# Five instead of six work pairs behind the first two scores of a run, and fewer double periods, in a fused attention and SwiGLU kernel

## The chip, the cores and the metric

The kernel runs on one core of a Trainium2 chip. The metric is the device time of one launch in microseconds (us); for the kernel before it is the median of three runs. Beside the times there is one profiled execution with its trace, from which all durations below come.

The engines of a core run side by side and wait for each other through semaphores: TensorE (PE in the profile; its weight loads are listed apart as PEld), VectorE (DVE), ScalarE (ACT), GpSimd (POOL), and SyncE (SP), which here mostly issues DMAs. What stands on one engine runs in the order in which the program wrote it.

## The reference

One sequence of 2048 rows with 512 features goes through two branches, which are mixed row by row by a gate. The batch dimension of 1 is left out below.

```python
g = sigmoid((x * gate_w).sum(-1, keepdims=True))
# branch a: attention with 32 heads of 16 features
qkv = (x @ wqkv).reshape(S, 3, 32, 16)          # q, k, v
p = softmax(q @ k.T * 16 ** -0.5)               # per head, 2048 x 2048
a = (p @ v) @ wo
# branch b: SwiGLU, hidden size 1792
b = (silu(x @ w1) * (x @ w3)) @ w2
out = g * a + (1 - g) * b
```

All inputs and the output are float32.

## The kernel before

**Attention in units.** Two heads are taken together, so there are 16 head pairs, and the 2048 queries are taken in two halves: 32 steps, each with one head pair and one half. A step has 16 blocks of 128 keys times two groups of 512 queries, that is 32 units, and there are 1024 units in all. One unit is:

- a score (letter Q, `score`, line 888): two matmuls, one for each head, with 50 rows of K as weights and 512 queries moving. The one sits in the upper half of the array's rows and the other in the lower half, so they run at the same time. They fill one of the two PSUM buffers named S (128 x 2 x 512);
- an exponential on ACT (line 892), over those 1024 columns at once, from S into a tile p in SBUF (twelve of them in rotation, four of which are named v). It follows the score in program order;
- two matmuls with V (line 875), p moving and 17 columns of V as weights, which add to the PSUM bank acc. The letter P (`pv`) does this for the two oldest pending units: four matmuls, which take four strips of the array's columns side by side. In the trace each such matmul is two records.

Since there are two S buffers, a score can only start when the exponential of the score two before it has been read out. The wait is on the score's weight load, which the trace lists under PEld and which in undisturbed work begins before the matmuls that stand ahead of it have ended.

**Work pairs.** Everything else that TensorE has to do (the rest of the projections, the three SwiGLU products, the output product) is cut into blocks whose contraction is split over the two halves of the array's rows. `feed()` (letter F) issues the next matmul of each half: a work pair, two matmuls of 64 rows by 512 columns that run side by side (lines 460, 584, 674, 681). Which block is next depends on how many letters have gone by (`clock`), since a bank must have been read by VectorE before it is written again.

**The order.** TensorE's program is a string of these letters, walked once at build time. A run of n units is

```python
run = lambda n, m=6: "QQ" + "F" * m + "QFFF" * (n - 3) + "Q" + "P" * (n // 2)
```

so two scores, m work pairs, then one score for each three work pairs, a last score, and all products with V of the run. The kernel has four runs of 8, then 15 times a run of 12 and two runs of 10 (32 units: one step), then `LONG` runs of 8, called long periods here. After them come `SHORT` double periods of 8 units (`two`), in which the products with V come in two groups with two scores between them:

```python
two = "QFFF" * 5 + "QPPQQPP"
```

A group of P stands between scores and work pairs in every run, one group in a long period and two in a double one. DMAs for the next step's K and Q (`load_step`), and the vector work on gates and sums, hang on the number of scores issued and of blocks done.

Of the kernel before, what the change touches and what calls it, by code (L numbers as in the profile page):

```python
# [17 lines left out]
P = 128  # L18
S = 2048
D = 512  # L20
F = 1792
# [13 lines left out]
def gated_mix_kernel(ctx: ExitStack, tc: tile.TileContext, x, wqkv, wo, w1, w3, w2, gate_w, out):  # L35
# [861 lines left out]


    NP = 8
    THIRDS, LONG, SHORT = 16, 35, 28  # L900
    run = lambda n, m=6: "QQ" + "F" * m + "QFFF" * (n - 3) + "Q" + "P" * (n // 2)
    two = "QFFF" * 5 + "QPPQQPP"
    order = run(8) * 4 + (run(12) + run(10) * 2) * (THIRDS - 1) + run(8) * LONG + "QQ" + "F" * 7 + two * SHORT + "QFFF" * 5 + "QPPPP"
    MORE = ["v0", "v1", "v2", "v3"]
    free = list(range(NP))

# [127 lines left out]
```

## Time and profile before

| | |
|---|---|
| median of 3 runs | 1396.81 us (1395.8 to 1397.53) |
| the profiled execution | 1396.22 us, of which 1394.4 us is the span from the first to the last instruction |
| PE | 1386.5 us busy, 99% of the span |
| PEld | 836.8 us, 60% |
| ACT | 1025.1 us, 74% |
| DVE | 491.5 us, 35% |
| POOL | 335.8 us, 24% |
| granted TensorE clock | 1.00 throughout |

Read the rows of the timeline so: start in us from the span's start, duration in us, engine, line, operation, tiles written and read, shape, how many such instructions follow one another, and in brackets the idle time of the engine ahead of them with what ended it. PE's busy time overlaps: a matmul is shown from its start to its (modelled) end, and the next one starts before that. What TensorE's work costs is therefore read from the distance between starts, and not from durations.

### The profile page before, as it was taken

The page shows a single profiled execution, that of the slowest core. Times are in us where ns is not written, and L with a number is a line of the kernel's source. Part 1 is how long each engine was busy: PE and PEld are TensorE (multiplying, and loading weights), DVE is VectorE, ACT ScalarE, POOL GpSimd, SP SyncE. Part 2 cuts the span into 40 slices and gives each one's busy share as a digit, 9 for nine tenths or more (in the row PEclk, how much of TensorE's full clock was granted, in tenths as well). Part 3 has the DMA queues.
Part 4 walks back from the last instruction along what each step waited for, and adds up shares of the span by engine and source line. Part 5 has one row for each costly group of instructions (what it writes and reads, how often), then busy time and mean ns, then how long its engine had stood idle before and what let it go on. Part 6 is the DMA issues. An engine that isn't in the chain of part 4 may idle for free.

```text
span 1394.4 us, 29335 instructions
## 1 busy us (share of the span) xinstructions
PE 1386.5 (99%) x11601; PEld 836.8 (60%) x11601; DVE 491.5 (35%) x1101; ACT 1025.1 (74%) x1151; POOL 335.8 (24%) x371
## 2 busy tenths in 40 slices
PE   9999999999999999999999999999999999999998
PEld 8766565656566565656565566566566555555554
DVE  6411111446464646564555545431111110110113
ACT  5467677777778677778777777777677787887884
POOL 6104344210111011101110114543253431232402
PEclk9999999999999999999999999999999999999999
DMA  9505455532323233332233424536534554444632
GB/s 272 139 10 144 98 145 142 120 94 62 77 71 91 60 80 78 76 86 71 62 78 77 107 67 108 122 107 124 110 105 91 118 123 88 96 100 98 162 110 84
DMA packets 111186, 141.30 MB, mean 101 GB/s; under 512 B 16422, under 2 KB 69414, under 8 KB 108066
## 3 DMA queue, kind: packets, MB, share of 16 engines
q1 hardware_dynamic: 109888, 137.40, 40.7%
q8 instruction: 93, 1.52, 0.5%
q10 hardware_dynamic: 1154, 1.97, 0.4%
q14 instruction: 51, 0.42, 0.1%
HBM read 90.69 MB, written 48.61 MB: 100 GB/s over the span
## 4 chain that ended last, share of the span: by engine, by line
PE 95%; DVE 1%; issue 0%; DVEq 0%
PE acc L875 33%; PE f L460 27%; PE S L888 19%; PE f L584 11%; PE f L674 2%; PE f L760 1%; PE f L681 1%; DVE xH L686 0%; DVE xL L686 0%; PE f L960 0%; DVE sg L497 0%; PE S L960 0%; DVE u L949 0%; DVE sg L515 0%; PE S L971 0%
## 5 line engine op out<-in xcount | busy, mean ns | idle before, releaser
L892 ACT ACTIVATE p<-S 128x1024 f32<-128x1024 f32 x864 | 817.2, 1027 | 273.6 <-PE S L888 272.2
L888 PE MATMUL S<-Qt,Kt 50*128 50x512 f32 x2048 | 409.9, 407 | 1.2 <-SPq L316 1.1
L875 PE MATMUL acc<-p,V 128*17 128x512 f32 x3456 | 400.8, 594 | 0.0
L888 PEld LDWEIGHTS S<-Qt,Kt 50*128 50x128 f32 x2048 | 187.8, 184 | 153.7 <-issue 73.0
L875 PEld LDWEIGHTS acc<-p,V 128*17 128x17 f32 x3456 | 88.7, 97 | 235.8 <-issue 235.1
L497 DVE RECIPROCAL sg<-sg 128x64 f32<-128x64 f32 x448 | 209.6, 518 | 52.6 <-issue 48.6
L460 PE MATMUL f<-xH,fl 64*128 64x512 f32 x1104 | 223.8, 394 | 0.1
L460 PE MATMUL f<-xH,fh 64*128 64x512 f32 x1104 | 221.6, 389 | 0.0
L460 PE MATMUL f<-xL,fh 64*128 64x512 f32 x1104 | 221.2, 389 | 0.0
L892 ACT ACTIVATE v<-S 128x1024 f32<-128x1024 f32 x160 | 153.0, 1027 | 54.7 <-PE S L888 54.4
L460 PEld LDWEIGHTS f<-xH,fh 64*128 64x128 f32 x1104 | 108.6, 184 | 23.3 <-DVE tick L847 0.2
L460 PEld LDWEIGHTS f<-xL,fh 64*128 64x128 f32 x1104 | 109.1, 187 | 22.4
L351 POOL CAST fh<-fr 128x512 fp32r<-128x512 f32 x35 | 22.1, 631 | 416.7 <-DMA fr<-in_B_w_dram 368.1
L460 PEld LDWEIGHTS f<-xH,fl 64*128 64x128 f32 x1104 | 108.8, 186 | 22.2 <-DVE raw L511 0.5
L847 DVE MEMSET tick<- 1x1 f32 x205 | 12.1, 59 | 310.4 <-PE f L584 152.5
L875 PE MATMUL acc<-v,V 128*17 128x512 f32 x640 | 77.1, 593 | 0.0
L584 PE MATMUL f<-xL,fh 64*128 64x512 f32 x208 | 66.2, 390 | 0.0
L584 PE MATMUL f<-xH,fl 64*128 64x512 f32 x208 | 65.9, 390 | 0.0
L584 PE MATMUL f<-xH,fh 64*128 64x512 f32 x208 | 61.2, 390 | 0.0
L857 DVE COPY u<-acc 128x512 f32<-128x512 f32 x31 | 21.5, 692 | 102.3 <-PE acc L875 102.3
L489 DVE COPY gs<-f 128x512 f32<-128x512 f32 x56 | 38.4, 687 | 53.2 <-PE f L460 52.4
L495 DVE TENSOR_SCALAR sg<-sg 128x512 f32<-128x512 f32 x56 | 26.1, 466 | 88.1 <-ACT sg L494 84.8
(221 smaller groups left out, 1417.2 us busy)
## 6 DMA issues: line engine op xcount, KB each, us to landing
Kt<-kH_d SPq DMA_DIRECT2D x124, 128.0 KB
h_d<-sg SPq DMA_DIRECT2D x56, 256.0 KB
sg<-h_d SPq DMA_DIRECT2D x43, 256.0 KB
fr<-in_B_w_dram SPq DMA_DIRECT2D x42, 256.0 KB
Qt<-qH_d SPq DMA_DIRECT2D x128, 64.0 KB
Kt<-kL_d SPq DMA_DIRECT2D x62, 128.0 KB
Qt<-qL_d SPq DMA_DIRECT2D x64, 64.0 KB
b_d<-yy SPq DMA_DIRECT2D x16, 256.0 KB
```

The source lines that it names most:

```text
L351: nc.gpsimd.tensor_copy(hi, src)
L460: return nc.tensor.matmul(ps, w[i == 1][r, k, :], (xL if i == 2 else xH)[b][r, k, :], start=n == 0 and not second, stop=n == 3 * ND - 1 an ...
L489: nc.vector.tensor_copy(gs, ps)
L495: small.append(lambda: nc.vector.tensor_scalar(sg, sg, 1.0, None, op0=OP.add))
L497: small.append(lambda q=q: nc.vector.reciprocal(sg[:, q:q + 64], sg[:, q:q + 64]))
L584: ins = nc.tensor.matmul(ps, hs[t][q][i == 1][r, P * o:P * o + P], (w2L if i == 2 else w2H)[q][r, o, :], start=n == 0 and not second, stop ...
L674: return nc.tensor.matmul(ps, ot[t][i == 1][r, P * k:P * k + P], wo_[k][i == 2][r, :], start=n == 0 and not second, stop=n == 3 * ND - 1 a ...
L681: return nc.tensor.matmul(ps, o_rows(t, k, i == 1)[r, :], wo_[k][i == 2][r, :], start=n == 0 and not second, stop=n == LATE - 1 and (secon ...
L857: nc.vector.tensor_copy(u, acc)
L875: nc.tensor.matmul(acc[r:r + DH + 1, :], V[:, k, 2 * j + h, :], p[:, h, :], start=k == 0, stop=k == NT - 1)
L888: nc.tensor.matmul(ps[:, h, :], Kt[i][r:r + 50, P * k:P * k + P], Qt[i][r:r + 50, t:t + 512], start=True, stop=True)
L892: nc.scalar.activation(p, ps, AF.Exp, scale=SCALE)
```

## The change

`run` gets five work pairs by default behind its first two scores. The four runs of the first step keep six. The pairs that this sets free, 45 in the runs of 12 and 10 and one in each long period, go where 16 double periods were: these become long periods, with 20 work pairs each instead of 15.

```diff
     NP = 8
-    THIRDS, LONG, SHORT = 16, 35, 28
-    run = lambda n, m=6: "QQ" + "F" * m + "QFFF" * (n - 3) + "Q" + "P" * (n // 2)
+    THIRDS, LONG, SHORT = 16, 51, 12
+    run = lambda n, m=5: "QQ" + "F" * m + "QFFF" * (n - 3) + "Q" + "P" * (n // 2)
     two = "QFFF" * 5 + "QPPQQPP"
-    order = run(8) * 4 + (run(12) + run(10) * 2) * (THIRDS - 1) + run(8) * LONG + "QQ" + "F" * 7 + two * SHORT + "QFFF" * 5 + "QPPPP"
+    order = run(8, 6) * 4 + (run(12) + run(10) * 2) * (THIRDS - 1) + run(8) * LONG + "QQ" + "F" * 7 + two * SHORT + "QFFF" * 5 + "QPPPP"
```

Scores, products with V and letters F are as many as before, counted from the string:

| stage | runs before | F before | runs now | F now |
|---|---|---|---|---|
| first step, runs of 8 | 4 | 84 | 4 | 84 |
| runs of 12 | 15 | 495 | 15 | 480 |
| runs of 10 | 30 | 810 | 30 | 780 |
| long periods (8 units) | 35 | 735 | 51 | 1020 |
| double periods (8 units) | 28 | 420 | 12 | 180 |
| the rest | | 22 | | 22 |
| sum | | 2566 | | 2566 |

Groups of P: 4 + 45 + 35 + 2 x 28 + 1 = 141 before, 4 + 45 + 51 + 2 x 12 + 1 = 125 now.

The first place is on TensorE in the second step, in the first run that the change reaches, around its third score. The pieces of the difference show work pairs (line 460, f<- a half of x and a half of a weight) and the score (line 888).

```order
 L460 MATMUL f<-xL_159,fh_5878 128x512
 L460 MATMUL f<-xL_479,fh_5872 128x512
+L888 MATMUL S<-Qt_109,Kt_112 128x512 x2
 L460 MATMUL f<-xH_158,fh_5878 128x512
 L460 MATMUL f<-xH_478,fh_5872 128x512
-L888 MATMUL S<-Qt_109,Kt_112 128x512 x2
```

The third score moves ahead of one work pair, and so does each later score of the run; the pair itself comes right behind it, ahead of the next score.

The second place is on TensorE at about the 870th of the 1024 units. Before, it lies in the double periods: two groups of products with V (line 875) with two scores between them.

```order
L888 MATMUL S<-Qt_109,Kt_112 128x512 x2
L875 MATMUL acc<-p_19348,V 17x512 x2
L875 MATMUL acc<-p_19353,V 17x512 x2
L875 MATMUL acc<-p_19376,V 17x512 x2
L875 MATMUL acc<-p_19387,V 17x512 x2
L888 MATMUL S<-Qt_109,Kt_112 128x512 x4
L875 MATMUL acc<-p_19404,V 17x512 x2
L875 MATMUL acc<-p_19423,V 17x512 x2
L875 MATMUL acc<-p_19448,V 17x512 x2
L875 MATMUL acc<-p_19469,V 17x512 x2
L888 MATMUL S<-Qt_109,Kt_112 128x512 x2
```

With the change the same stretch lies in the long periods: the eight units' products come in one group, and the next run's first two scores stand behind all of them.

```order
L888 MATMUL S<-Qt_109,Kt_112 128x512 x2
L875 MATMUL acc<-p_19487,V 17x512 x2
L875 MATMUL acc<-p_19492,V 17x512 x2
L875 MATMUL acc<-p_19508,V 17x512 x2
L875 MATMUL acc<-p_19525,V 17x512 x2
L875 MATMUL acc<-p_19544,V 17x512 x2
L875 MATMUL acc<-p_19555,V 17x512 x2
L875 MATMUL acc<-p_19576,V 17x512 x2
L875 MATMUL acc<-p_19587,V 17x512 x2
L888 MATMUL S<-Qt_109,Kt_112 128x512 x4
```

There is one change between scores and products in place of two for these eight units, and the two scores that stood between the groups now stand at a run's head.

## The prediction

> **What bounds the kernel now.** I read the page first: the busy times, the shares of the chain that ended last, and the two groups that the change touches.
>
> ```profile
> PE 1386.5 (99%) x11601; PEld 836.8 (60%) x11601; DVE 491.5 (35%) x1101; ACT 1025.1 (74%) x1151; POOL 335.8 (24%) x371
> ...
> PE 95%; DVE 1%; issue 0%; DVEq 0%
> ...
> L892 ACT ACTIVATE p<-S 128x1024 f32<-128x1024 f32 x864 | 817.2, 1027 | 273.6 <-PE S L888 272.2
> L888 PE MATMUL S<-Qt,Kt 50*128 50x512 f32 x2048 | 409.9, 407 | 1.2 <-SPq L316 1.1
> ```
>
> TensorE is the bound, and 95% of the last chain lies on it. A busy PE does not say that it runs at its beat, though: a score that waits for its buffer shows under PEld, at its weight load. So the waits of PEld come next, and beside them those of ACT on itself.
>
> ```profile
> PEld S L888 <- issue: 73.0, 85, 1.5
> PEld S L888 <- ACT p L892: 49.8, 65, 0.9
> ACT p L892 <- ACT p L892: 0.7, 4, 0.2
> ACT v L892 <- ACT v L892: 0.3, 2, 0.2
> ACT p L892 <- ACT v L892: 0.2, 1, 0.2
> ```
>
> The first two rows look like 123 us of waiting and are mostly something else. 85 is the number of all groups of P outside the double periods (141 - 56), and 73.0 / 85 is 0.86 us each: the weight loader is idle behind a group of P, since the products keep the array. The double periods' 56 groups make 56 x 0.86 = 48 of the 49.8 us in the second row, put down to ACT only because its signal came last. What is left for real waits on an exponential is about 2 us. So today TensorE hardly ever waits for ACT, and its time is the number of its items times their beat, plus what it costs to go from scores to products and back. Both are read from the timeline, from one group of P to the same place of the next period: a long period, then a double one.
>
> ```profile
> 945.12 3.63 PE L875 MATMUL acc<-p,V 128*17 128x512 f32 x32
> ...
> 950.64 0.40 PE L888 MATMUL S<-Qt,Kt 50*128 50x512 f32 x2
> ...
> 955.28 0.39 PE L888 MATMUL S<-Qt,Kt 50*128 50x512 f32 x2
> 955.60 3.63 PE L875 MATMUL acc<-p,V 128*17 128x512 f32 x32
> ```
> ```profile
> 1122.44 1.91 PE L875 MATMUL acc<-p,V 128*17 128x512 f32 x16
> ...
> 1124.95 1.91 PE L875 MATMUL acc<-p,V 128*17 128x512 f32 x16
> ...
> 1131.85 1.91 PE L875 MATMUL acc<-p,V 128*17 128x512 f32 x16
> ```
>
> From 950.64 to 955.28 there are 20 items (5 scores, 15 work pairs): 4.64 / 20 = 0.232 us an item. A long period takes 955.60 - 945.12 = 10.48 us for 8 scores, 21 pairs and 4 P, a double one 1131.85 - 1122.44 = 9.41 us for 8 scores, 15 pairs and 4 P. Six pairs fewer should save 6 x 0.232 = 1.39 us, and only 1.07 are saved: the second group of P (at 1124.95) costs 0.32 us.
>
> **Part one: fewer groups of P.** All letters stay as many as they were (1024 scores, 2566 F, 512 P), so the items' beat alone gives no change. Groups of P go from 141 to 125: 16 x 0.32 = 5.1 us less, on the engine that sets the end. This is the whole possible gain.
>
> **Part two: the third score comes one pair sooner, in 96 runs** (45 of 12 and 10 units, 51 long periods). Whether its buffer is free by then is the question. The head of a run with six pairs:
>
> ```profile
> 711.59 0.73 PE L888 MATMUL S<-Qt,Kt 50*128 50x512 f32 x4
> 712.19 3.82 ACT L892 ACTIVATE p<-S 128x1024 f32<-128x1024 f32 x4 [4.16 <-PE S L888]
> 713.32 0.19 PEld L888 LDWEIGHTS S<-Qt,Kt 50*128 50x128 f32 x2
> 713.55 0.40 PE L888 MATMUL S<-Qt,Kt 50*128 50x512 f32 x2
> 713.78 0.40 PE L460 MATMUL f<-xH,fl 64*128 64x512 f32 x2
> ```
>
> The first exponential starts at 712.19 and, at the page's mean of 1.027, ends at 713.22. The third score's weight load goes out at 713.32, 0.10 us later, and the next work pair starts at 713.78, 0.46 us after the load. With five pairs the load would be due at 713.09, and the buffer is not free. What a late exponential does to a score stands elsewhere, where ACT paused and the loads met it:
>
> ```profile
> 717.96 0.19 PEld L888 LDWEIGHTS S<-Qt,Kt 50*128 50x128 f32 x2
> 718.03 1.94 ACT L892 ACTIVATE v<-S 128x1024 f32<-128x1024 f32 x2 [0.17 <-ACT v L892]
> 718.19 0.39 PE L888 MATMUL S<-Qt,Kt 50*128 50x512 f32 x2
> 718.42 0.40 PE L460 MATMUL f<-xH,fl 64*128 64x512 f32 x2
> ...
> 719.11 0.19 PEld L888 LDWEIGHTS S<-Qt,Kt 50*128 50x128 f32 x2 [0.26 <-ACT v L892]
> 719.12 0.49 PE L888 MATMUL S<-Qt,Kt 50*128 50x512 f32 x2
> ...
> 719.45 0.39 PE L460 MATMUL f<-xH,fl 64*128 64x512 f32 x2
> ```
>
> The exponential that began at 718.03 ended at 719.06, and the load went out at 719.11: 0.05 us behind. From this load to the next pair it is 0.34 us instead of 0.46, so a late load gives 0.12 us of its lead back; the pair comes at 719.45 where four items after 718.42 it would have been 719.35. By these numbers the third score with five pairs loads at 713.22 + 0.05 = 713.27, and the pair behind it starts at 713.61 instead of 713.78 - 0.23 = 713.55. 0.06 us is lost at each run's third score, between 0.05 and 0.06 within the rows' last digit: 96 x 0.055 = **5.3 us** (4.8 to 5.8), which alone takes back the 5.1.
>
> **Part three: the rest of such a run.** From the third score on the loads go out right behind the exponentials, with no lead. Two trains of before ran in this way, one behind another pause of ACT and one in the last run, where too few pairs stood ahead of a score:
>
> ```profile
> 642.78 7.44 ACT L892 ACTIVATE p<-S 128x1024 f32<-128x1024 f32 x8 [0.20 <-ACT v L892]
> 643.86 0.19 PEld L888 LDWEIGHTS S<-Qt,Kt 50*128 50x128 f32 x2 [0.26 <-ACT p L892]
> ...
> 644.89 0.40 PE L888 MATMUL S<-Qt,Kt 50*128 50x512 f32 x2
> ...
> 648.63 0.40 PE L888 MATMUL S<-Qt,Kt 50*128 50x512 f32 x2
> ```
> ```profile
> 1372.22 5.62 ACT L892 ACTIVATE p<-S 128x1024 f32<-128x1024 f32 x6 [0.57 <-PE S L888]
> ...
> 1373.30 0.19 PEld L888 LDWEIGHTS S<-Qt,Kt 50*128 50x128 f32 x2 [0.45 <-ACT p L892]
> ...
> 1374.34 0.39 PE L888 MATMUL S<-Qt,Kt 50*128 50x512 f32 x2
> ...
> 1376.21 0.39 PE L888 MATMUL S<-Qt,Kt 50*128 50x512 f32 x2
> ```
>
> Eight exponentials in 7.44 us follow one another every (7.44 - 1.03) / 7 = 0.916 us, less than a score and three pairs take undisturbed (718.19 - 713.55 over 5 intervals: 0.928), so ACT catches up by itself and no second wait follows. But the scores come every (648.63 - 644.89) / 4 = 0.935 us in the first train and (1376.21 - 1374.34) / 2 = 0.935 in the second: 0.008 more than 0.927 to 0.928. I can't say from the trace why, and take it as measured, for all intervals but the first behind a wait. After the third score a run of 8 has 5 intervals, one of 10 has 7, one of 12 has 9: 51 x 4 + 30 x 6 + 15 x 8 = 504, times 0.008 is **4.0 us**. The ends are 0 (the extra is chance in two trains) and 600 x 0.008 = 4.8.
>
> The Trainium skill speaks harder against the change. Its page "ScalarE: Activation LUTs", section "What ACT_TABLE_LOAD costs", gives an activation with immediate operands 186 ns + 0.833 ns a column and lets neighbours overlap by 93 ns; by an estimate from that page, 1024 columns would follow one another every 0.946 us, more than TensorE's 0.927, and with no slack left each of the 600 intervals would lose 0.019: 11.4 us in place of 4.0, and 1408.5 us in all. The two trains' 0.916 above, and 1.94 - 1.03 = 0.91 for the pair at 718.03, don't bear that out.
>
> **Part four: ACT's pauses.** The waits of ACT on itself list 4 + 2 + 1 = 7 pauses of up to 0.2 us. Before, one cost 0.10 on PE, as at 719.45. With no lead in hand it costs its whole 0.2 where more scores of the run follow: 7 x 0.1 = 0.7 us more (0 to 1.9, were each 0.27).
>
> What moves without a price: the pairs from 16 double periods lie in long periods now, with the same beat; VectorE's and GpSimd's work and SP's loads for the next step hang on the same counts and change places by single items, covered by a DVE at 35% and by loads that no row of the waits names ahead of a score. If that cover were gone, a score would show a wait on a DMA.
>
> **The sum.** Against the profiled execution's own 1396.22 us: -5.1 + 5.3 + 4.0 + 0.7 = +4.9, so **1401.1 us**. The ends are -5.1 + 4.8 = -0.3 (1395.9) and -5.1 + 5.8 + 4.8 + 1.9 = +7.4 (1403.6). The profiled execution lies 0.6 below the median of 1396.81, well inside the runs' 1395.8 to 1397.53.
>
> **The rivals.**
> - *The wait alone.* The third score is late, but later scores keep 0.928 and pauses cost as before: -5.1 + 5.3 = 1396.4, up to 1397.1 with the pauses. For it: 0.008 comes from six intervals in two trains. Against: both trains show the same 0.935. Chance 0.22.
> - *No wait at all, and faster.* The place is the weight load of the third score, the price is nothing, and all of the 5.1 stays: 1391.1. It decides if the first exponential ends 0.06 us sooner against the scores, for instance if the load could follow its end at once and not by 0.05. For it: a late load already gives back 0.12. Against: the load at 1373.30 in the last run, which came 1.08 after the exponential's start at 1372.22, just as at 719.11. Chance 0.10.
> - *ACT sets the pace of whole runs.* A run with five pairs lasts as long as one with six, and each freed pair is paid twice: 96 x 0.232 = 22.3 lost against 5.1, 1413.4. It decides when exponentials follow one another more slowly than 0.928. Against: 0.916, and 272.2 us in which ACT waited for scores. Chance 0.05. The 0.946 of the Trainium skill, above, would lie between this and the forecast.
> - *The pairs don't fill what is freed.* Were F letters left empty, work would go behind the loop. The order has as many work pairs inside the loop as before, so I give it no more than 0.03, with no time other than that of no change.
>
> **How the numbers follow.** A measurement of this kernel can tell about 0.2%, 2.8 us, from no change: slower means above 1399.6. The forecast has 0.60, of which 0.05 lies below that mark. So slower is 0.55 + 0.05 (ACT's pace) = 0.60, the same 0.05 + 0.22 + 0.03 = 0.30, faster 0.10. The forecast's own range is 1395.9 to 1403.6. The range for 8 in 10 takes the wait alone in and leaves out 1391.1 and 1413.4: 1395 to 1404.
>
> **What will show it.** Each run's third score from the second step on has a weight load 0.05 us behind the first exponential's end, with an idle time put down to ACT, near 96 more such rows than now; a long period takes 10.48 - 0.23 + 0.06 + 0.03 = 10.34 us; scores in it come every 0.935; the waits put down to "issue" ahead of a score's load become 101. If long periods take 10.25, there is no wait, and 1391.1 has it; at 10.30 the later scores keep their beat; at 10.48 ACT paces. The prediction is wrong in kind if the double periods' second group of P turns out to be worth something other than 0.32.

## The result and the profile after

The kernel with the change takes **1405.54 us** (median, 1403.35 to 1405.73), beside 1396.74 us for the kernel before on the same chip (1395.8 to 1397.53). The ratio is 1.006, with a 95% interval of 1.0049 to 1.0072. It is slower, as forecast, but by 8.8 us instead of 4.9, and the time lies above the predicted range of 1395 to 1404. The profiled execution of the changed kernel took 1405.73 us, with a span of 1403.9 us.

The page of the changed kernel, in the places that were shown of the kernel before:

```profile
PE 1394.2 (99%) x11601; PEld 817.0 (58%) x11601; DVE 491.9 (35%) x1101; ACT 1014.9 (72%) x1151; POOL 334.7 (24%) x371
...
PE 94%; DVE 1%; POOL 0%; ACT 0%; issue 0%; DVEq 0%; POOLq 0%
...
L892 ACT ACTIVATE p<-S 128x1024 f32<-128x1024 f32 x864 | 809.9, 1044 | 291.8 <-PE S L888 291.3
L888 PE MATMUL S<-Qt,Kt 50*128 50x512 f32 x2048 | 411.0, 412 | 1.2 <-DVEq L316 1.1
```

Nothing here stands out: TensorE is still 99% busy, and the instructions are as many as before. POOL, ACT and POOLq are new in the chain's shares, with 0% each. The waits of PEld and of PE say more; the columns are the total in us, the number of waits and the longest.

```profile
PEld S L888 <- issue: 86.6, 101, 1.5
PEld S L888 <- ACT p L892: 44.8, 140, 0.9
PEld S L888 <- ACT v L892: 4.5, 20, 0.5
PEld f L584 <- POOL fl L548: 2.5, 1, 2.5
PE f L584 <- POOL fl L548: 2.1, 1, 2.1
```

The first row has 101 entries, as predicted for 125 groups of P less 24 in the double periods. Of the second row's 140, 24 belong to the double periods, and 116 are left where there were 65 - 56 = 9; the third row, of the tiles named v, has 20 where there were 4. So 136 loads of a score are listed as waiting for an exponential where there were 13: the 96 third scores that were forecast, 32 fourth scores, and 8 others. (These lists name only idle times above 0.15 us.) The last two rows of the list are one event, and no such row stood in the waits of before: a work pair of the third SwiGLU product (line 584) waited 2.1 us for GpSimd. The prediction had no such wait.

One long period in the timeline of the changed kernel, from the two scores at its head to its group of P:

```profile
743.45 0.73 PE L888 MATMUL S<-Qt,Kt 50*128 50x512 f32 x4
...
744.05 7.44 ACT L892 ACTIVATE p<-S 128x1024 f32<-128x1024 f32 x8 [2.90 <-PE S L888]
...
745.13 0.19 PEld L888 LDWEIGHTS S<-Qt,Kt 50*128 50x128 f32 x2 [0.22 <-ACT p L892]
...
745.19 0.45 PE L888 MATMUL S<-Qt,Kt 50*128 50x512 f32 x2
...
746.05 0.18 PEld L888 LDWEIGHTS S<-Qt,Kt 50*128 50x128 f32 x2 [0.16 <-ACT p L892]
746.17 0.40 PE L888 MATMUL S<-Qt,Kt 50*128 50x512 f32 x2
...
746.96 0.19 PEld L888 LDWEIGHTS S<-Qt,Kt 50*128 50x128 f32 x2
...
747.34 0.40 PE L460 MATMUL f<-xL,fh 64*128 64x512 f32 x2
...
749.91 0.40 PE L888 MATMUL S<-Qt,Kt 50*128 50x512 f32 x2
```

The third score's load waits 0.22 us for the first exponential, and goes out 1.08 us after that one's start (744.05 to 745.13), the interval the prediction used. The eight exponentials take 7.44 us again, so ACT could follow faster than the scores come, which is every (749.91 - 746.17) / 4 = 0.935 us. These two signs are as forecast. The fourth score's load waits as well (0.16 us), where the prediction said that no second wait follows. Over all periods of a kind, from the starts of the scores in the traces (medians, us):

| kernel | run of 12 | run of 10 | long period | third score, long period | interval of later scores, long period |
|---|---|---|---|---|---|
| before | 15.905 | 13.195 | 10.480 | 1.969 | 0.928 |
| before, less a pair of 0.232 | 15.673 | 12.963 | 10.248 | 1.737 | 0.928 |
| after | 15.842 | 13.075 | 10.354 | 1.789 | 0.937 |

The third score is counted from the first score's start to its own end, less the 0.39 us of an undisturbed one, because a late one's record is longer (0.45 above). The long period was forecast at 10.34 and is 10.354. Double periods are unchanged (9.414 against 9.413). So the regular part of the forecast holds, and what is missing must lie in single places. Among the 51 long periods two stand out: the one that begins at 930.59 lasts 14.215 us, 3.86 too long, and the one at 888.62 lasts 10.940, 0.59 too long. The first holds the wait for GpSimd.

### The place where it was lost

In the timeline of the changed kernel, SP issues a store of the hidden product (line 516), then the next step's loads (lines 300, 293 and 305: six for Q, six for K and two for m, 14 in all), then the load of the same hidden product in another layout (line 546); GpSimd splits that into fh and fl (lines 547 and 548), and work pairs read these.

```profile
924.34 0.33 SPq L516 DMA_DIRECT2D h_d<-sg  x1
924.75 0.38 SPq L300 DMA_DIRECT2D Qt<-qH_d  x1
...
930.28 0.57 SPq L305 DMA_DIRECT2D Qt<-m_d  x2
930.95 2.16 SPq L546 DMA_DIRECT2D fr<-h_d  x2
...
936.37 0.40 PE L584 MATMUL f<-xH,gw 64*128 64x512 f32 x2
...
936.84 0.61 POOL L547 CAST fh<-fr 128x512 fp32r<-128x512 f32 x1 [15.98 <-PE f L584]
...
937.53 1.26 POOL L548 TENSOR_TENSOR fl<-fr,fh 128x512 fp32r<-128x512 f32 x1
...
938.85 0.79 PE L584 MATMUL f<-xH,fl 64*128 64x512 f32 x1 [2.08 <-POOL fl L548]
...
940.42 4.46 PE L875 MATMUL acc<-p,V 128*17 128x512 f32 x32
```

The load of h_d is issued 6.6 us after its store (930.95 - 924.34), the split ends at 938.79, and the pair that is due at 936.60 starts at 938.85. The group of P behind it takes 4.46 us where it took 3.63 before. In the kernel before, the same chain reads:

```profile
900.26 0.33 SPq L516 DMA_DIRECT2D h_d<-sg  x1
900.69 0.99 SPq L546 DMA_DIRECT2D fr<-h_d  x2
...
904.09 0.61 POOL L547 CAST fh<-fr 128x512 fp32r<-128x512 f32 x1 [4.40 <-DMA fr<-h_d]
...
904.78 1.27 POOL L548 TENSOR_TENSOR fl<-fr,fh 128x512 fp32r<-128x512 f32 x1
...
911.98 0.39 PE L584 MATMUL f<-xH,fl 64*128 64x512 f32 x1
...
933.96 0.42 SPq L300 DMA_DIRECT2D Qt<-qH_d  x1
```

There the load follows the store by 0.43 us, the split is done 5.8 us after the store (906.05), and the pair comes 11.7 us after it. In the changed kernel the pair is due 12.3 us after its store, so there was no less room, but the split took 14.45 us, 8.66 more than before. 6.18 us of these are the later issue (6.61 against 0.43 behind the store). Most of the rest, 2.5 us, lies between the issue of the load and the start of the split: 5.89 us (930.95 to 936.84) against 3.40 (900.69 to 904.09). The row at 936.84, where the split starts, names a matmul as what ended GpSimd's idle time; that matmul ended 0.07 us ahead of it, and the load landed at 936.74. With the old 3.40 us the split would, by an estimate from these rows, have been done at 936.3, just in time. So both parts made the wait: the load was issued behind the 14 others, and it took longer behind them. The loads of the next step, which stood 33 us behind this hand-over, stand inside it now.

They moved because the two hang on different counts. The step's loads are issued at a number of scores (behind the 21st score of a step in this part of the program, `issued % 32 == 21`); the hidden product's store and load come with the work pairs. At this place the changed order has issued 64 fewer work pairs by a given score: 45 from the runs of 12 and 10, 19 from the long periods up to there. 64 pairs are some three runs. Counted in the traces, the store goes out behind the 637th score before and behind the 661st now, and the next step's loads are due behind the 661st in both.

### The profile page after: what moved, and what is told of

It is laid out like the page before. It is cut to its first block, busy times and chain, and to the rows that moved or that the text cites. A ratio compares the mean times of both kernels' runs of the same rounds, so it can differ in the third digit from the quotient of the medians.

```text
span 1403.9 us, 29331 instructions
## 1 busy us (share of the span) xinstructions
PE 1394.2 (99%) x11601; PEld 817.0 (58%) x11601; DVE 491.9 (35%) x1101; ACT 1014.9 (72%) x1151; POOL 334.7 (24%) x371
## 4 chain that ended last, share of the span: by engine, by line
PE 94%; DVE 1%; POOL 0%; ACT 0%; issue 0%; DVEq 0%; POOLq 0%
PE acc L875 32%; PE f L460 27%; PE S L888 19%; PE f L584 11%; PE f L674 2%; PE f L760 1%; PE f L681 1%; DVE xH L686 0%; DVE xL L686 0%; PE f L960 0%; DVE sg L515 0%; DVE sg L497 0%; POOL fl L548 0%; ACT v L892 0%; PE S L960 0%
## 5 line engine op out<-in xcount | busy, mean ns | idle before, releaser
L888 PEld LDWEIGHTS S<-Qt,Kt 50*128 50x128 f32 x2048 | 184.2, 184 | 190.6 <-issue 86.6
L460 PE MATMUL f<-xH,fl 64*128 64x512 f32 x1104 | 219.9, 392 | 0.0
L460 PEld LDWEIGHTS f<-xH,fh 64*128 64x128 f32 x1104 | 105.5, 186 | 20.2 <-DVE gs L489 0.5
L460 PEld LDWEIGHTS f<-xL,fh 64*128 64x128 f32 x1104 | 105.6, 186 | 19.4
L460 PEld LDWEIGHTS f<-xH,fl 64*128 64x128 f32 x1104 | 105.6, 186 | 18.9
L584 PE MATMUL f<-xH,fl 64*128 64x512 f32 x208 | 66.6, 394 | 2.1 <-POOL fl L548 2.1
L584 PE MATMUL f<-xH,raw 64*128 64x512 f32 x192 | 55.2, 392 | 0.0
```

The lines of the kernel that those rows point to most:

```text
L460: return nc.tensor.matmul(ps, w[i == 1][r, k, :], (xL if i == 2 else xH)[b][r, k, :], start=n == 0 and not second, stop=n == 3 * ND - 1 an ...
L584: ins = nc.tensor.matmul(ps, hs[t][q][i == 1][r, P * o:P * o + P], (w2L if i == 2 else w2H)[q][r, o, :], start=n == 0 and not second, stop ...
L888: nc.tensor.matmul(ps[:, h, :], Kt[i][r:r + 50, P * k:P * k + P], Qt[i][r:r + 50, t:t + 512], start=True, stop=True)
```

## The experiments

The theory after this reading: 4.4 of the 8.8 us are a collision on SP, which the order alone caused, and the rest is the prediction's own sum. The rivals: the whole 8.8 us is the wait for exponentials and its pace (the collision would then cost little, as other work would fill it), or the groups of P are worth less than 0.32 each.

### The next step's loads ahead of the hand-over

The change, with the step's loads behind the 14th score instead of the 21st in this one step, so that they come before the store:

```diff
-            if issued % 32 == (22 if 128 <= issued < 160 else 14 if issued < 640 else 21 if issued < 672 else 6) and step < 2 * NPAIR:
+            if issued % 32 == (22 if 128 <= issued < 160 else 14 if issued < 672 else 6) and step < 2 * NPAIR:
```

> The changed kernel with one edit: the next step's K and Q (13 DMAs on SP) are issued seven scores sooner in the one step where they stood right ahead of the last two pieces of the hidden product's first operand. Theory (the 2.1 us wait and the slower products behind it, 3.9 us in one long period near 930 us, come from the order on SP): the wait is gone, that period is as long as the others (10.35), 1405.5 - 3.9 = 1401.6 (1400.6 to 1402.6). Rival (the hidden product's store itself comes too late, since 64 fewer work pairs stand ahead of the same score): the wait stays in size within 1 us, 1404.5 to 1405.8.

Measured: **1401.18 us** (1400.54 to 1401.91), a ratio to before of 1.0033 (1.002 to 1.0045). The timeline of SP in this kernel:

```profile
906.33 0.38 SPq L300 DMA_DIRECT2D Qt<-qH_d  x1
...
912.14 0.57 SPq L305 DMA_DIRECT2D Qt<-m_d  x2
...
924.09 0.34 SPq L516 DMA_DIRECT2D h_d<-sg  x1
924.53 0.99 SPq L546 DMA_DIRECT2D fr<-h_d  x2
```

The load follows its store by 0.44 us again, and the wait for GpSimd is gone. 4.4 us of the change's 8.8 are gone with it, by one number that moves 14 DMAs. In two more kernels with the same shift, below, the same edit was worth 3.2 us (1400.41 to 1397.21) and 5.1 us (1396.16 to 1391.04).

The same edit was made to the kernel before, where nothing stands in the hand-over:

> The kernel before with the edit of the load order alone: the next step's K and Q are issued seven scores sooner in that one step, where they stood behind the hidden product's pieces anyway. Theory (the order matters only where the step's 13 DMAs stand right ahead of those pieces): no change, 1396.6 (1395.8 to 1397.6). Rival (loading a step sooner at that place is worth something by itself, so that the 4 us of the changed kernel were not its own): 1392.6.

Measured: 1396.24 us (1395.49 to 1396.68) beside 1396.21, 0.9999 (0.9989 to 1.0008). So the edit brings nothing by itself; it only takes the collision away.

### The collision from the other side

If the collision comes from the shift of pairs against scores and not from late scores, a shift the other way may cause it too, in a kernel in which no score waits. This is the kernel before with seven pairs instead of six in 42 of the 45 runs of 12 and 10, paid for by 7 more double periods:

```diff
-    THIRDS, LONG, SHORT = 16, 35, 28
+    THIRDS, LONG, SHORT = 16, 28, 35
...
-    order = run(8) * 4 + (run(12) + run(10) * 2) * (THIRDS - 1) + run(8) * LONG + "QQ" + "F" * 7 + two * SHORT + "QFFF" * 5 + "QPPPP"
+    order = run(8) * 4 + (run(12, 7) + run(10, 7) * 2) * (THIRDS - 2) + run(12) + run(10) * 2 + run(8) * LONG + "QQ" + "F" * 7 + two * SHORT + "QFFF" * 5 + "QPPPP"
```

> The kernel before, changed the other way: seven instead of six pairs behind the first two scores in 42 of the 45 runs of 12 and 10, and 28 long and 35 double periods instead of 35 and 28, so seven more groups of products with V and no score that comes sooner. Theory (a group of products costs 0.32 us and nothing else changes): 1396.7 + 7 x 0.32 = 1399.0 (1398.3 to 1399.8). Rival (the groups were not what the double periods cost, and the 16 fewer of the change saved nothing): 1396.7.

Measured: 1403.49 us (1402.29 to 1403.52), 1.0047 (1.003 to 1.0063): 4.5 us above what was expected. The run was meant to price groups of P, and its forecast had no collision. Its timeline has one:

```profile
889.17 0.33 SPq L516 DMA_DIRECT2D h_d<-sg  x1
889.59 0.39 SPq L300 DMA_DIRECT2D Qt<-qH_d  x1
...
896.40 0.57 SPq L305 DMA_DIRECT2D Qt<-m_d  x2
897.07 0.94 SPq L546 DMA_DIRECT2D fr<-h_d  x2
...
904.07 0.50 PE L584 MATMUL f<-xH,fl 64*128 64x512 f32 x1 [2.92 <-POOL fl L548]
```

The pairs are 42 ahead of the scores here instead of 64 behind, and the 14 loads land in a hand-over again. This long period is 4.91 us too long. Taken out of 1403.49 it leaves 1398.6, near the expectation. That the collision has nothing to do with the five pairs as such is thereby shown. The store goes out behind the 621st score here, and a step's loads are due behind the 622nd and the 661st; the order before, with its store behind the 637th, lay between the two.

### The wait moved to the end of the run

The changed kernel again, but with six pairs behind the first two scores, and one pair fewer ahead of the last score of a run instead. Groups of P and the shift stay as in the change.

```diff
-    run = lambda n, m=5: "QQ" + "F" * m + "QFFF" * (n - 3) + "Q" + "P" * (n // 2)
+    run = lambda n, m=6, g=2: "QQ" + "F" * m + "QFFF" * (n - 4) + "Q" + "F" * g + "Q" + "P" * (n // 2)
...
-    order = run(8, 6) * 4 + ...
+    order = run(8, 6, 3) * 4 + ...
```

> The changed kernel with six pairs behind the first two scores again and the missing pair taken from the last gap of the run instead (two pairs ahead of the last score), so one score of a run is late as before, but no score follows it. Theory (scores behind a late one come every 0.936 instead of 0.927 because their weight loads have no lead): the 5.6 us of pace in 96 runs go, 0.06 per run stays, 1405.5 - 5.6 = 1399.9 (1398.7 to 1401). Rival (the slower pace belongs to the changed program as a whole, as its mean matmul of 392 to 393 ns against 389 would also have it): 1405.5 with scores every 0.936 still.

Measured: 1400.41 us (1399.6 to 1402.93), 1.003 (1.002 to 1.0039). A long period of its timeline:

```profile
743.62 0.40 PE L888 MATMUL S<-Qt,Kt 50*128 50x512 f32 x2
...
747.32 0.40 PE L888 MATMUL S<-Qt,Kt 50*128 50x512 f32 x2
...
747.98 0.19 PEld L888 LDWEIGHTS S<-Qt,Kt 50*128 50x128 f32 x2 [0.23 <-ACT p L892]
748.02 0.45 PE L888 MATMUL S<-Qt,Kt 50*128 50x512 f32 x2
```

There is still one late load per run, now the last, but no score comes after it: (747.32 - 743.62) / 4 = 0.925 us for those before. The long period is 10.314 us by the median: 0.066 above the 10.248 of a run with a pair less, and 0.040 below the change's 10.354. So the scores come more slowly only behind a late one. The collision is there as before (a wait of 2.31 us for fl), and its long period is 4.07 too long.

With both edits, the late score last and the step's loads first:

> The changed kernel with both edits that helped: the missing pair taken from the last gap of the run, and the next step's K and Q issued ahead of the hidden product's last store in the one step where they clashed. Theory (the two losses are independent): 1400.4 - 4.1 = 1396.3 (1395.3 to 1397.5), level with the kernel before: 5.2 us of groups saved against 96 x 0.06 for scores that come too soon. Rival (the load order hides another wait that shows once this one is gone): 1398 to 1400.

Measured: 1397.21 us (1396.47 to 1399.04) beside 1396.57, 1.0005 (0.9996 to 1.0015). Without collision and without a slower pace, the change is level with the kernel before. The runs of 12, 10 and 8 show 96 times 0.065 us on top of a run with a pair less, 6.2 us, against 16 groups of P at 0.32, 5.1 us.

### No wait, by a shorter first exponential

To see what the 16 groups are worth without any late load, each run's first exponential from the second step on was taken over 448 of 512 columns of each head; the other 64 are filled with something else by a small copy on ACT ahead of it, so this kernel leaves an eighth of that exponential out. (The condition also finds one exponential in each of the 12 double periods and one ahead of them; `i_` is the place in the order, so that the condition finds the first Q of a run.)

```diff
-        nc.scalar.activation(p, ps, AF.Exp, scale=SCALE)
+        w = 448 if issued >= 32 and order[i_:i_ + 2] == "QQ" else 512
+        if w < 512:
+            nc.scalar.activation(p[:, :, w:512], ident.rearrange("p (h t) -> p h t", h=2), AF.Copy)
+        nc.scalar.activation(p[:, :, 0:w], ps[:, :, 0:w], AF.Exp, scale=SCALE)
```

> The changed kernel in which the first exponential of each run from the second step on covers 448 of each head's 512 columns; the other 64 are filled with a constant by a small copy ahead of it, while ACT is idle, so the weights of these keys are wrong there and the output with them. The first exponential ends about 0.1 us sooner. Theory (the third score's wait is the cause of both the late score and the slower pace behind it): both go, 6.1 + 5.6 us, 1405.5 - 11.7 = 1393.8 (1392.5 to 1395.5), with the 3.9 us near 930 us still in it. Rival 1 (only the wait itself goes): 1399.4. Rival 2 (the late score is not due to the exponential): 1405.5.

Measured: 1396.16 us (1393.48 to 1397.01), 0.9994 (0.9984 to 1.0004). This is above the range expected and below both rivals. The long period is 10.273 us, so the wait is nearly gone; the runs together are 8.9 us shorter than in the change where 11.7 had been expected, since some 0.025 us stay in each. The collision is there as expected (3.89 us in one period). With the step's loads first as well:

> The changed kernel with the shortened first exponential (448 of 512 columns per head, the rest a constant, so these weights and the output are wrong) and the same edit of the load order. Theory (16 groups of products fewer save 5.2 us, and the third score's wait and the load order are all that is lost): 1396.2 - 3.9 = 1392.3 (1391.3 to 1393.5), faster than the kernel before. Rival (the fewer groups save less than 0.32 each): 1394 to 1396.

Measured: **1391.04 us** (1390.45 to 1391.27), 0.996 (0.9945 to 0.9974), 0.3 us below the range expected: the edit brought 5.1 us instead of 3.9. Waits, and the same long period in the timeline, where the line of the exponential is now 895:

```profile
PEld S L888 <- issue: 86.8, 101, 1.8
PEld S L888 <- ACT p L895: 11.9, 19, 0.9
PEld S L888 <- ACT p L894: 10.2, 12, 0.9
```
```profile
738.20 7.37 ACT L895 ACTIVATE p<-S 128x896 f32<-128x896 f32 x8 [2.65 <-PE S L888]
...
739.17 0.19 PEld L888 LDWEIGHTS S<-Qt,Kt 50*128 50x128 f32 x2
...
739.40 0.40 PE L888 MATMUL S<-Qt,Kt 50*128 50x512 f32 x2
```

The load goes out 0.97 us after the exponential's start instead of 1.08, and no idle time is listed ahead of it; the 140 waits for ACT are down to 19 + 12, of which 24 are those of the double periods. In this kernel the runs of 12, 10 and 8 are longer than those of before less a pair by 15 x 0.025 + 30 x 0.024 + 51 x 0.026 = 2.4 us; the losses that stand in single odd runs fall from 2.1 us in the trace of before to 0.6, and the program's head and tail are 0.7 us shorter. Its span is 4.95 us less than before's, so the groups are worth 4.95 + 2.4 - 1.5 - 0.7 = 5.15 us: 16 x 0.32, as forecast. This sum is made of the same durations as the forecast's 0.32, so it closes the account and doesn't measure the price a second time; what does is the whole time, 1391.04, against the rival's 1394 to 1396. The rival that these groups are worth less falls.

### Each part of the runs alone

The kernel before with five pairs in 42 of the 45 runs of 12 and 10 alone, and with five pairs in the long periods alone; each buys 7 groups of P:

```diff
-    THIRDS, LONG, SHORT = 16, 35, 28
+    THIRDS, LONG, SHORT = 16, 42, 21
...
+    order = run(8) * 4 + (run(12, 5) + run(10, 5) * 2) * (THIRDS - 2) + run(12) + run(10) * 2 + run(8) * LONG + ...
```
```diff
-    THIRDS, LONG, SHORT = 16, 35, 28
+    THIRDS, LONG, SHORT = 16, 42, 21
...
+    order = run(8) * 4 + (run(12) + run(10) * 2) * (THIRDS - 1) + run(8, 5) * LONG + ...
```

> The kernel before with five pairs in 42 of the 45 runs of 12 and 10 only, the long periods keep six, and 42 long and 21 double periods. Theory: seven groups fewer, -2.3; 28 runs of 10 lose 0.11 and 14 runs of 12 lose 0.14 to 0.17, +5.3; the hidden product's store shifts by two runs, to between two steps' loads, so no clash: 1396.7 + 3.0 = 1399.7 (1398.5 to 1400.7). Rival (any shift of pairs against scores at that place costs 4 us more): 1403.7.

> The kernel before with five pairs in the long periods only, 42 long and 21 double periods. Theory: seven groups fewer, -2.3; 42 long periods of 10.354 where 10.249 would be the items' beat, +4.4; 16 pairs later at the hidden product's store, less than a run, no clash with a step's loads: 1396.7 + 2.1 = 1398.8 (1397.8 to 1399.8). Rival (any shift of pairs against scores there costs 4 us more): 1402.8.

Measured: 1397.99 us (1397.21 to 1398.48), 1.0011 (1.0001 to 1.0021), and 1397.82 us (1396.96 to 1398.73), 1.0008 (0.9999 to 1.0018), beside 1396.57. The first came out 1.7 us below what was expected and outside its range, the second 1.0 below and inside. The regular part is as expected: in the first the 28 runs of 10 take 13.073 and the 14 of 12 take 15.811, which is 28 x 0.110 + 14 x 0.138 = 5.0 us more than a pair less would give, and 7 groups take back 2.3. What the expectation had left out are, by these traces, the single odd runs: together 2.1 us in the trace of before, 0.6 here. 5.0 - 2.3 - 1.5 = +1.2, where +1.4 was measured. In the second it is 42 x 0.099 - 2.3 - 0.7 = +1.2, where +1.25 was measured. These single losses move with every order, by one or two us either way, and no view of before gave a forecast of them.

## Why the prediction was right in kind and wrong in size

**The failed step** is in the paragraph on what moves without a price: that SP's loads for the next step "change place by single items", under cover of a VectorE at 35% and of waits that named no load. They did not move by single items: where the pairs of 45 runs and 19 long periods had been taken out, everything that hangs on pairs lay 64 pairs, some three runs, later against everything that hangs on scores. On SP's queue this put 14 DMAs between a store and the load that follows it, and on TensorE a work pair, not a score, waited for it. The paragraph's own sign ("a score would show a wait on a DMA") would not have shown it. The price is 4.4 us by the run with the loads first (1405.54 against 1401.18), and no term of the sum covered it.

In the profiled execution the 3.86 us of that long period divide into 2.25 us between the starts of two pairs (936.37 to 938.85, less one item), some 0.8 for three slow items (938.85 to 940.42) and 0.83 for the group of P (4.46 against 3.63). More than 40% of these 3.86 us is thus TensorE's lower clock behind the wait, not the wait.

**Part one, the groups of P**, held: 5.15 us for 16, forecast 5.1.

**Part two, the third score**, held: in the kernel with the loads first it comes at 1.794, 1.792 and 1.818 us in runs of 8, 10 and 12, against 1.737 to 1.740 less a pair, which is 51 x 0.057 + 30 x 0.052 + 15 x 0.078 = 5.64 us; forecast 5.3, at most 5.8. The runs of 12 lose more than the others, which I had not seen.

**Part three, the pace**, held with a size a little too small: in the same kernel the runs' whole excess is 51 x 0.102 + 30 x 0.110 + 15 x 0.138 = 10.57 us, of which 4.93 are left for the 504 intervals, 0.0098 each; forecast 0.008 and 4.0, at most 4.8. That the slower pace comes from late loads is shown (0.925 where the late load is the last one, 0.928 to 0.929 where the first exponential is shorter and hardly any load is late). What the part had wrong is that "no second wait follows". The idle times ahead of the loads, read from the traces without a lower limit, and the distance from a load to the next work pair say so (medians over the long periods):

| score of the long period | 3rd | 4th | 5th | 6th | 7th | 8th |
|---|---|---|---|---|---|---|
| idle ahead of its load, before (us) | 0.043 | 0.045 | 0.038 | 0.045 | 0.038 | 0.045 |
| idle ahead of its load, after | 0.219 | 0.148 | 0.122 | 0.104 | 0.086 | 0.073 |
| its load to the next pair, before | 0.460 | 0.460 | 0.460 | 0.460 | 0.460 | |
| its load to the next pair, after | 0.338 | 0.365 | 0.389 | 0.404 | 0.422 | |

After the change every load of the period, and not only the third, goes out 0.05 us behind the end of the exponential two before it; before it was 0.10 to 0.12. The lead that the third load lost comes back by some 0.02 us a score, since ACT follows a little faster (0.90 to 0.92 us from start to start) than the scores come (0.93 to 0.94); in runs of 12 the distance is back at 0.460 at the ninth score. In the rows above, the fifth score is such a one (746.96 to 747.34, 0.38 us, and no wait listed). So the pace is slow while the loads' lead is short. Why a short lead puts the items behind it some 2 ns further apart each (0.0098 us for four) stays open. The Trainium skill's 0.946 us between exponentials ("ScalarE: Activation LUTs", section "What ACT_TABLE_LOAD costs"), which the prediction had weighed, isn't seen here: eight take 7.44 us, 0.916 apart.

**Part four, ACT's pauses**, can't be told apart. Forecast at +0.7, it disappears in the single odd losses, which went down by 1.0 us with the loads first.

**The sum.** With the loads first, -5.15 + 10.6 - 1.0, and 0.4 more at the program's head and tail, make +4.8, where the spans differ by 4.9 and the medians by 4.5; the prediction's +4.9 and 1401.1 us are met by the measured 1401.18 of that kernel. So close a match is in part luck: parts two and three were 0.3 and 0.9 too small, and part four, head and tail together came out 1.3 below the forecast's 0.7. The change itself has 4.4 more. Of the rivals, "no wait at all" has its price right, by the run at 1391.04, and its condition does not hold: the load has to go out sooner than it does, as in that run, where the first exponential is shorter. "The wait alone" is what the kernel with the late score last shows, at 1397.21 without the collision, beside the 1396.4 to 1397.1 that the rival gave. ACT doesn't pace whole runs: a long period would have stayed at 10.48. And no work pairs were left over for the end: the traces have as many of their matmuls ahead of the last score as before (5287 records).

The smaller odd period (0.59 us at 888.62) is another single loss: a work pair waited for a read by VectorE. It is in the kernel with the loads first too (0.55), so it is part of that kernel's time and not of the 4.4. The kernels with the shorter first exponential have the same shift of pairs and nothing above 0.11 us in a long period but the collision, so the shift alone doesn't make it; its cause is not shown.

```profile
894.40 0.98 PE L460 MATMUL f<-xH,fh 64*128 64x512 f32 x2
...
894.88 0.18 PEld L460 LDWEIGHTS f<-xH,fh 64*128 64x128 f32 x1 [0.53 <-DVE gs L489]
```

None of the kernels that leave nothing out is faster than the kernel before. Six pairs taken from runs buy one group of P, 0.32 us. A taken pair costs 0.065 us where the late score is the last of the run, and 0.052 to 0.078 and the slower pace besides where it is the third: 6.2 or 10.6 us for 96 pairs, against 5.15.

## What to carry to other kernels

Where some events hang on one count and some on another, a change of the order moves all of one kind against all of the other, by the sum of what was moved ahead of that place. So count the shift at each hand-over (a store, the load behind it, the split and the reader) and look what else stands on the same queue within that shift; a list of waits that names no such load says only that there was room in the order before. And price a gap on TensorE with the slower clock that may follow it, which in the profiled execution was two fifths of the loss.

## What the runs showed of the hardware

A gap of about 2 us without matmuls was followed by 3.41 us at half of TensorE's clock. The windows of the changed kernel around the wait (us; busy time and instructions of PE, PEld, DVE, ACT and POOL; the granted clock; the share and rate of the DMA engines):

```profile
935.32:938.73 3.41, 1.45 (x14) 0.83 (x10) 0.06 (x1) 2.40 (x3) 1.81 (x2) 1.00 0.75 219
938.73:942.14 3.41, 3.29 (x18) 1.18 (x22) 0.00 (x0) 1.52 (x2) 3.25 (x6) 0.50 0.33 79
942.14:945.55 3.41, 3.41 (x34) 1.19 (x28) 2.07 (x4) 0.14 (x2) 1.64 (x2) 1.00 0.00 0
```

The clock is full in the gap itself, 0.50 for 3.41 us from about when work resumes, and full again. The other two kernels of this shift show the same 3.41 us, one behind a gap of 1.94 us, where the low clock sets in 0.7 us after the work has resumed (timeline and window of the kernel with the shorter first exponential):

```profile
931.75 0.50 PE L584 MATMUL f<-xH,fl 64*128 64x512 f32 x1 [1.94 <-POOL fl L548]
```
```profile
932.43:935.84 3.41, 3.41 (x20) 0.66 (x20) 1.25 (x3) 1.85 (x3) 3.25 (x5) 0.50 0.27 79
```

The kernel with seven pairs has the same behind its gap of 2.92 us (905.81 to 909.22). A gap of up to 1.63 us at the program's start (58.6 to 60.3 us, in the kernel with seven pairs) lowered no clock. The gap doesn't cost the clock in every execution either: 3.41 us at 0.50 would make the mean clock of an execution 0.999, and two of the changed kernel's five have 1.000. They are its two shortest, 1403.35 and 1404.77 us, against 1405.54 to 1405.73. This may be why the same edit was worth 3.2 us in one kernel and 5.1 in another. How long the wait was in executions other than the profiled ones is not shown.

The Trainium skill ("TensorE: Matmul & The Clock Gate", section "Why this matters for your kernels") asks for no idle gaps above some 3 us between bursts of matmuls. The gaps here are shorter and cost the clock all the same. The 3.41 us of slow clock behind them agree with the window of about 3.4 us that the page gives for getting back up (section "What's actually happening"). I had no run that varies the gap's length, so from what length on this happens is not shown beyond these gaps.

A score's late load leaves its mark on the scores that follow it, as the prediction had read it from two stretches of the trace before: 0.935 to 0.937 us between scores instead of 0.925 to 0.928, and the loads behind it stay late by less and less, up to the ninth score in a run of 12. The kernel in which only the last score is late loses nothing of this kind.
